# The last 128 tokens of a two-product kernel, computed and stored in three column parts

## The chip, the cores and the metric

The kernel runs on one core of a Trainium2 chip. A core has five engines that run side by side: TensorE (matrix products), VectorE, ScalarE, GpSimd and SyncE (called SP here, which does nothing in this kernel but issue transfers). They share a memory of 128 partitions (SBUF). TensorE writes its results to a second small memory, PSUM, from which VectorE or ScalarE copy them out. Transfers (DMAs) between SBUF and the chip's main memory are issued by an engine's queue and carried out by 16 DMA engines. The metric is the device time of one execution in microseconds (us). Five runs of the kernel before took 341.65 to 343.1 us, with a median of 342.26.

## The reference

The computation is an attention whose keys and values begin with a few extra "beacon" rows, followed by a two-layer network with a squared ReLU:

```
k_all = concatenate([beacon_k, k]); v_all = concatenate([beacon_v, v])
a     = softmax(scale * q @ k_all^T, causal over k)        # 8 batches, 8 heads, 576 rows, 64 wide
x     = (a @ v_all), heads side by side                    # 4608 tokens x 512
h     = x @ w_in                                           # first product, 512 -> 2048
g     = relu(h) ** 2
out   = g @ w_out                                          # second product, 2048 -> 512, float32
```

The output has 4608 rows (tokens) of 512 columns.

## The kernel before

The network's part goes through the 4608 tokens in nine chunks of 512 (`TCH`, `NCH`). The function `add_chunk(j)` describes the work of chunk `j` as a list of operations. In the first product (line 845) 16 groups of four matmuls each give 128 of the 2048 hidden columns for 512 tokens. ScalarE or VectorE apply the ReLU to each group (lines 861 and 863), and VectorE squares two of them at a time (line 870) into the tile `g`. The second product (line 880) takes four token tiles of 128 tokens. Each is the sum of 16 matmuls of 128x512 in one PSUM bank (`ps`), in four quarters (`qd`) of four matmuls. Each matmul has a weight load of its own, since the weights are the 128 tokens of `g`, and the 512 columns of `w_out` are what streams past them. The bank is then copied to the tile `osb` (the operation `ev`, which the function `copy_on` gives as line 316 on ScalarE or line 318 on VectorE), and a store (`st`) is issued from SP. In all chunks but the end of the last, two token tiles go out in one store of 512 KB (line 908). The last two token tiles of the last chunk have a store of 256 KB each (line 906).

The order of all the work is worked out when the kernel is built. The class `Order` plays through a small model of the engines: each operation has engines it may run on, a duration, a priority (lower goes first), the operations it needs (`deps`), those that must merely have been started (`behind`), and perhaps a PSUM bank to take and later give back. At each moment, a free engine takes the ready operation of the lowest priority. An operation counts as seen by those that need it a little after its end (`LAT`, 0.2 us for TensorE). The instructions are then written out in that order, and each engine runs its own in it. What waits on what on the chip is derived from which data each instruction reads and writes.

The operations that the change concerns are these: the quarters `s2.{j}.{ts}.{qd}` have the priority `base + 100 + 4 * ts + qd` and need the quarter before; the copy `ev{j}.{ts}` has the priority -15 and may run on ScalarE or, if that is busy, VectorE; the store `st{j}.{ts}` has the priority -20 and runs on SP. There are four PSUM banks in the pool `ps`, and the tile `osb` has two buffers of two token tiles each. SP's queue carries all stores and, earlier in the kernel, most loads. ScalarE's queue issues only two loads, at the very start (line 513). Line 1007 stands for what closes the kernel: SP waits for the transfers, and the engines meet.

Of the kernel before, what the change touches and what calls it, by code (L numbers as in the profile page):

```python
# [45 lines left out]
class Order:  # L46
# [16 lines left out]
    def add(self, *a, **kw):  # L63
        op = Op(*a, **kw)
        op.need = [d for d in op.need if d is not None]
        self.ops.append(op)
        return op
# [126 lines left out]
def kernel(  # L194
# [11 lines left out]
    nc = tc.nc  # L206
# [8 lines left out]
    TCH = 512  # L215
    NCH = n_tokens // TCH
    NMC = d_model // 128
    NFT = d_ff // 128
# [5 lines left out]
    def sb(name, shape, dt):  # L224
        return pool.tile(shape, dt, name=name)
# [5 lines left out]
    w_out_sb = sb("w_out", [128, NFT, d_model], BF16)  # L231
# [36 lines left out]
    g = [sb(f"g{i}", [128, NFT, TCH], BF16) for i in range(2)]  # L268
    osb = [sb(f"osb{i}", [128, 2, d_model], FP32) for i in range(2)]
# [3 lines left out]
    ps = [psum.tile([128, 512], FP32, name=f"ps{i}") for i in range(4)]  # L273
# [16 lines left out]
    add = order.add  # L290
# [23 lines left out]
    def copy_on(e, dst, src):  # L314
        if e == "ACT":
            nc.scalar.copy(dst, src)  # L316
        else:
            eng[e].tensor_copy(dst, src)  # L318
# [237 lines left out]
    for pr, segs in enumerate(STREAM):  # L556
        off, at = {}, 0
        for c, t0, t1 in segs:
# [3 lines left out]
            while t0 < t1:  # L562
                n, o = divmod(PW * pr + at, 512)
                w = min(t1 - t0, 512 - o)
                PIECES[n].append((pr, c, t0, t0 + w, o))
                t0, at = t0 + w, at + w
# [183 lines left out]
    s2_ops = {}  # L750
# [4 lines left out]
    def feeds_of(lo, hi):  # L755
        return [o for o, l, h in fed if l < hi and h > lo]
# [44 lines left out]
    w_ops = {}  # L801
# [9 lines left out]
    def add_weights_out():  # L811
        for i in range(4):
# [4 lines left out]
                    in_=moe_w_out.rearrange("(c p) f -> p c f", p=128)[:, i * n:(i + 1) * n, :])]  # L817
            w_ops["out", i] = add(f"wout{i}", "POOL", 1.3, emit, prio=-90 + i, behind=[v_loads[1][4]] if i == 0 else [w_ops["out", i - 1]], dma=2.6)

    def add_chunk(j):  # L820
        base = 1.0e5 + 1000.0 * j
        G = g[j % 2]
        sq = []
        t0, t1 = j * TCH, (j + 1) * TCH
        wrap = t1 // RING * RING
        if j == 0 and NSPLIT:
            parts = [(0, SPLIT[0].hi), (SPLIT[0].hi, t1)]
        else:
            parts = [(t0, t1)]
        for n, (lo_, hi_) in enumerate(parts):  # L830
            s1_ops[lo_, hi_] = []
        for f in range(NFT // 2):
            sqs = []
            for n, (lo_, hi_) in enumerate(parts):
                spans = [(lo_, wrap), (wrap, hi_)] if lo_ < wrap < hi_ else [(lo_, hi_)]
                N = hi_ - lo_
                relus = []
                for ft in (2 * f, 2 * f + 1):
                    box = {}

                    def emit_s1(e, ft=ft, spans=spans, box=box):
                        h = ps[box["s1"].held[2]]
                        for lo, hi in spans:
                            for mc in range(NMC):
                                nc.tensor.matmul(h[:, lo - spans[0][0]:hi - spans[0][0]],  # L845
                                                 w_in_sb[:, mc, ft * 128:(ft + 1) * 128],
                                                 xT[:, mc, lo % RING:lo % RING + hi - lo],
                                                 start=(mc == 0), stop=(mc == NMC - 1))

                    s1 = add(f"s1.{j}.{ft}.{n}", "PE", 0.865 * N / TCH, emit_s1, prio=base + ft + 0.5 * n,  # L850
                             deps=feeds_of(lo_, hi_) + [w_ops["in", f // 2]]
                             + [s2_ops[j - 2, u] for u in range(4) if j >= 2],
                             take=("ps", "mlp"), pe_time=0.865 * N / TCH)
                    box["s1"] = s1
                    s1_ops[lo_, hi_].append(s1)

                    def emit_relu(e, ft=ft, lo=lo_ - t0, hi=hi_ - t0, box=box):
                        h = ps[box["s1"].held[2]][:, 0:hi - lo]
                        dst = G[:, ft, lo:hi]
                        if e == "ACT":  # L860
                            nc.scalar.activation(dst, h, AF.Relu, bias=0.0, scale=1.0)  # L861
                        else:
                            nc.vector.tensor_scalar(out=dst, in0=h, scalar1=0.0, scalar2=None, op0=ALU.max)  # L863

                    relus.append(add(f"relu{j}.{ft}.{n}", ("ACT", "DVE"), {"ACT": 0.2 + N / 1200.0, "DVE": 0.13 + N / 960.0},
                                     emit_relu, prio=-20.0, deps=[s1], give=s1))

                def emit_sq(e, f=f, lo=lo_ - t0, hi=hi_ - t0):
                    d = G[:, 2 * f:2 * f + 2, lo:hi]
                    nc.vector.tensor_tensor(out=d, in0=d, in1=d, op=ALU.mult)  # L870

                sqs.append(add(f"sq{j}.{f}.{n}", "DVE", 0.1 + 0.6 * N / TCH, emit_sq, prio=-10.0, deps=relus))
            sq.append(sqs)
        for ts in range(TCH // 128):
            prev, first = None, {}
            for qd in range(4):
                def emit_s2(e, ts=ts, qd=qd, first=first):
                    o = ps[first["s2"].held[2]]
                    for fc in range(4 * qd, 4 * qd + 4):
                        nc.tensor.matmul(o, G[:, fc, ts * 128:(ts + 1) * 128],  # L880
                                         w_out_sb[:, fc, :], start=(fc == 0), stop=(fc == NFT - 1))

                prev = add(f"s2.{j}.{ts}.{qd}", "PE", 0.865, emit_s2, prio=base + 100 + 4 * ts + qd,
                           deps=sq[2 * qd] + sq[2 * qd + 1] + [w_ops["out", qd], prev],
                           take=None if qd else ("ps", "mlp"), pe_time=0.865)
                first.setdefault("s2", prev)
            s2_ops[j, ts] = prev
            u = 2 * j + ts // 2
            last = u == 2 * NCH - 1

            def emit_ev(e, ts=ts, first=first, u=u):
                copy_on(e, osb[u % 2][:, ts % 2, :], ps[first["s2"].held[2]])

            deps = [prev]
            if u >= 2:
                deps += st_ops[u - 2]
            evs = evs if ts % 2 else []
            evs.append(add(f"ev{j}.{ts}", ("ACT", "DVE"), {"ACT": 0.62, "DVE": 0.66}, emit_ev, prio=-15.0, deps=deps,
                           give=first["s2"]))
            st_ops.setdefault(u, [])  # L900
            if last or ts % 2:
                def emit_st(e, u=u, ts=ts, last=last):
                    d = osb[u % 2]
                    if last:
                        t0 = u * 256 + 128 * (ts % 2)
                        nc.sync.dma_start(out=out[t0:t0 + 128, :], in_=d[:, ts % 2, :])
                    else:
                        nc.sync.dma_start(out=out[u * 256:u * 256 + 256, :].rearrange("(t p) d -> p t d", p=128), in_=d)

                st_ops[u].append(add(f"st{j}.{ts}", "SP", 0.65, emit_st, prio=-20.0, deps=evs[-1:] if last else evs,  # L910
                                     dma=0.7 if last else 1.4))

    st_ops = {}
# [6 lines left out]
    for b in range(B):  # L920
# [8 lines left out]
        for n, (x, c) in enumerate(([] if b < NPE else nat) + [("v", c) for c in range(NT)]):  # L929
            behind, sync = [], []  # L930
            if x == "v" and b == 0:
                pass
            elif x == "v" and b == 1 and c == 0:
                behind = [strided[1, 0, HP - 1, "q"]]
            elif b == 2 and n == 0:
                sync = [w_ops["out", 3]]
            elif b >= NPE and x == "v" and c == 0:
                for y in "qk":
                    add_trans(b, y, lp - 5.0)
                behind = trans[b, "q"] + trans[b, "k"]  # L940
# [19 lines left out]
        if b >= 1:  # L960
            for j in late:
                add_chunk(j)
            late = []
# [48 lines left out]
```

## Time and profile before

| | us |
|---|---|
| median of 5 runs | 342.26 |
| the profiled execution | 342.79 |
| its span, first to last instruction | 340.7 |
| TensorE busy | 331.6 (97% of the span) |
| ScalarE busy | 190.4 |
| VectorE busy | 171.5 |
| GpSimd busy | 91.4 |
| last stretch of the second product (line 880) | 323.00 to 336.83 |
| last copy out of PSUM (line 316) | 336.91 to 337.49 |

The profile is of one execution, taken by the hardware's own profiler. The difference between the execution's own time and the span (2.1 us) lies outside the first and last instruction. TensorE's clock was granted in full. The page of the profile lists groups of instructions by source line and engine: the output tile, the input tiles, the shapes, how many there were, the time in which one of them ran, the mean length in ns of one, and the idle time ahead of them with what ended it. Other views give the instructions of a stretch in order of time, the chain of work that ended last, followed back from the last instruction, and the packets that the DMA engines moved, in 40 slices of a stretch, with each queue's number of packets. Queue q1 is SP's and q10 is ScalarE's. A matmul's length in these views runs from its start to the end of its last column; since matmuls are pipelined, the distance between two starts is shorter than that.

### The profile page before, as it was taken

What the parts mean: (1) busy time and instruction counts of PE and PEld (TensorE: products, weight loads), DVE (VectorE), ACT (ScalarE), POOL (GpSimd) and SP (SyncE); (2) the same over time, 40 slices, a digit from 0 to 9 for tenths busy, and PEclk for the clock granted to TensorE, in tenths of its full rate; (3) what the DMA queues carried; (4) which work ended last, traced back from release to release, by engine and by line L of the source; (5) the groups of instructions that cost most, each with busy time, mean ns of one, the idle gap of its engine ahead of it and who ended that gap; (6) DMA issues with size and microseconds to landing.
All of it is one profiled execution on the core that took longest, in us unless ns stands there. A gap on an engine that the chain in (4) does not pass through costs nothing.

```text
span 340.7 us, 7674 instructions
## 1 busy us (share of the span) xinstructions
PE 331.6 (97%) x3123; PEld 184.8 (54%) x3165; DVE 171.5 (50%) x388; ACT 190.4 (56%) x269; POOL 91.4 (27%) x145
## 2 busy tenths in 40 slices
PE   8999999999999999999999999989999999999995
PEld 7687765544554554555468854545554544444442
DVE  4886876237556972586347644664265403301300
ACT  3976865377548745675557544674367216515711
POOL 9874803316404504051424041313000000000000
PEclk9999999999999999999999999999999999999999
DMA  8999989999999998899989994998310131011002
GB/s 144 210 195 218 202 138 203 224 244 212 193 213 239 183 192 166 180 236 184 186 167 228 186 204 98 238 220 161 99 62 2 34 99 62 0 63 62 0 32 93
DMA packets 143665, 51.72 MB, mean 152 GB/s; under 512 B 130670, under 2 KB 138382, under 8 KB 143630
## 3 DMA queue, kind: packets, MB, share of 16 engines
q1 hardware_dynamic: 135231, 42.25, 62.7%
q0 software_dynamic: 7904, 8.69, 15.0%
q8 instruction: 25, 0.41, 0.5%
q10 hardware_dynamic: 495, 0.30, 0.3%
q14 instruction: 10, 0.08, 0.1%
HBM read 37.22 MB, written 9.44 MB: 137 GB/s over the span
## 4 chain that ended last, share of the span: by engine, by line
PE 82%; DMA 10%; POOL 4%; SPq 2%; issue 1%; ACT 0%; DVE 0%; POOLq 0%; ACTq 0%
PE ps L880 34%; PE ps L845 32%; PE ps L715 7%; PE strip L611 7%; DMA qk_area<-in_k_dram 3%; DMA stg<-in_k_dram 2%; DMA stg<-in_v_dram 2%; DMA kT<-qk_area 2%; SPq L765 2%; POOL qk_area L440 1%; DMA stg<-in_q_dram 1%; PE ps L475 1%; PE ps L782 1%; POOL stg L362 1%; POOL w_in L807 0%
## 5 line engine op out<-in xcount | busy, mean ns | idle before, releaser
L845 PE MATMUL ps<-xT,w_in 128*128 128x512 bf16 (+3 forms) x689 | 132.7, 340 | 0.9 <-issue 0.2
L880 PE MATMUL ps<-w_out,g 128*128 128x512 bf16 x549 | 130.5, 379 | 1.7 <-issue 0.5
L620 ACT ACTIVATE pt<-strip 128x1024 bf16<-128x1024 f32 (+3 forms) x107 | 101.9, 1000 | 43.0 <-PE strip L611 42.6
L845 PEld LDWEIGHTS <-w_in 128*128 128x128 bf16 x704 | 65.5, 98 | 52.0 <-issue 1.1
L861 ACT ACTIVATE g<-ps 128x512 bf16<-128x512 f32 (+2 forms) x120 | 67.5, 563 | 44.5 <-PE ps L845 43.7
L870 DVE TENSOR_TENSOR g<-g 128x1024 bf16<-128x1024 bf16 (+2 forms) x80 | 52.8, 665 | 68.5 <-ACT g L861 67.6
L880 PEld LDWEIGHTS <-g 128*128 128x128 bf16 x576 | 52.5, 98 | 57.4 <-issue 1.7
L318 POOL CAST qk_area<-stg 128x512 bf16<-128x512 f32 (+2 forms) x60 | 39.5, 667 | 66.8 <-DMA stg<-in_q_dram 34.4
L318 POOL CAST vb<-stg 128x512 bf16<-128x512 f32 (+1 forms) x40 | 25.7, 649 | 70.9 <-DMA stg<-in_v_dram 51.0
L316 ACT COPY osb<-ps 128x512 f32<-128x512 f32 x27 | 15.8, 586 | 51.1 <-PE ps L880 43.3
L715 PEld LDWEIGHTS <-pt 128*128 128x128 bf16 (+1 forms) x960 | 35.7, 98 | 11.0 <-issue 1.9
L715 PE MATMUL ps<-vb,pt 128*128 128x65 bf16 (+1 forms) x960 | 39.8, 194 | 0.1
L689 DVE TENSOR_TENSOR pt<-pt,tri 128x512 bf16<-128x512 bf16 x64 | 30.8, 490 | 10.7 <-ACT pt L620 9.6
L611 PE MATMUL strip<-qT,kT 64*128 64x208 bf16 (+15 forms) x596 | 34.2, 239 | 0.8 <-DMA kT<-qk_area 0.8
L734 DVE TENSOR_TENSOR xn<-ps,rcp 128x320 bf16<-128x320 f32 (+2 forms) x64 | 31.5, 492 | 2.3
L611 PEld LDWEIGHTS <-kT 64*128 64x128 bf16 x596 | 19.0, 94 | 22.1 <-issue 18.8
L732 DVE RECIPROCAL rcp<-ps 128x5 f32<-128x5 f32 (+2 forms) x64 | 12.2, 191 | 35.8 <-PE ps L715 35.6
L863 DVE TENSOR_SCALAR g<-ps 128x512 bf16<-128x512 f32 (+2 forms) x40 | 23.5, 602 | 9.8 <-PE ps L845 8.0
L318 DVE COPY osb<-ps 128x512 f32<-128x512 f32 x9 | 6.2, 691 | 17.9 <-PE ps L880 17.7
L286 PE MATMUL ps<-g 128*128 128x256 bf16 (+1 forms) x83 | 11.0, 285 | 1.1 <-DVE warm L293 1.1
L362 POOL DMA_DIRECT2D stg<-in_v_dram x10 | 8.6, 866 | 5.5 <-DMA w_in<-in_moe_w_in_dram 4.0
L693 DVE TENSOR_TENSOR pt<-pt,tri 80x160 bf16<-80x160 bf16 x32 | 9.8, 307 | 0.0
(38 smaller groups left out, 72.8 us busy)
## 6 DMA issues: line engine op xcount, KB each, us to landing
out_dram<-osb SPq DMA_DIRECT2D x17, 512.0 KB, 3.8
stg<-in_q_dram SPq DMA_DIRECT2D x24, 256.0 KB, 5.1
stg<-in_k_dram SPq DMA_DIRECT2D x18, 256.0 KB, 5.1
stg<-in_v_dram SPq DMA_DIRECT2D x18, 256.0 KB, 4.9
w_in<-in_moe_w_in_dram POOLq DMA_DIRECT2D x4, 512.0 KB, 7.8
w_out<-in_moe_w_out_dram POOLq DMA_DIRECT2D x4, 512.0 KB, 11.3
stg<-in_v_dram POOLq DMA_DIRECT2D x6, 256.0 KB, 7.9
stg<-in_k_dram SPq DMA_DIRECT2D x6, 224.0 KB, 4.6
```

Source lines behind the costliest of these rows:

```text
L316: nc.scalar.copy(dst, src)
L318: eng[e].tensor_copy(dst, src)
L611: nc.tensor.matmul(st[:, hj, at:at + t1 - t0], kT[b % 2][hp, pr, 128 * c:128 * c + 128], qT[b % 2][hp, pr, t0:t1], start=True, stop=True,)
L620: nc.scalar.activation(pt[:, :, at:at + width], strips[qk.slots[s]][:, :, 0:width], AF.Exp, bias=0.0, scale=scale)
L689: nc.vector.tensor_tensor(out=d, in0=d, in1=tri[:, m0:m0 + m, :][:, None].to_broadcast([128, 2, m, 128]), op=ALU.min)
L715: nc.tensor.matmul(a[:, at + (t - tl[0]) * (D + 1):at + (t - tl[0] + 1) * (D + 1)], P[0:rr, hj, o:o + 128], vb[b % 2][0:rr, c, 2 * pr + hj ...
L734: nc.vector.tensor_tensor(out=xn[b % 2].rearrange("p t (h d) -> p h t d", d=D)[:, h0:h0 + nh, tl[0]:tl[0] + nt], in0=a[:, :, :, 0:D], in1= ...
L845: nc.tensor.matmul(h[:, lo - spans[0][0]:hi - spans[0][0]], w_in_sb[:, mc, ft * 128:(ft + 1) * 128], xT[:, mc, lo % RING:lo % RING + hi - lo],
L861: nc.scalar.activation(dst, h, AF.Relu, bias=0.0, scale=1.0)
L863: nc.vector.tensor_scalar(out=dst, in0=h, scalar1=0.0, scalar2=None, op0=ALU.max)
L870: nc.vector.tensor_tensor(out=d, in0=d, in1=d, op=ALU.mult)
L880: nc.tensor.matmul(o, G[:, fc, ts * 128:(ts + 1) * 128], w_out_sb[:, fc, :], start=(fc == 0), stop=(fc == NFT - 1))
```

## The change

A new function, `add_last`, takes the place of the operations of the last token tile of the last chunk. The 512 output columns are computed in three parts of 256, 128 and 128 columns. Each part is a sum of 16 matmuls in a PSUM bank of its own, again in four quarters. The quarters follow one another by `behind` and not by `deps`, and a part's first quarter follows the last quarter of the part before. The first part is copied out by ScalarE, the second by VectorE, the third by ScalarE. Each has a store of its own, of 128 rows by its columns; the first two are issued from SP, the last from ScalarE's queue. The other three token tiles are as before.

```diff
+    def add_last(j, ts, base, sq):
+        u = 2 * NCH - 1
+        for n, (lo, hi) in enumerate(((0, 256), (256, 384), (384, 512))):
+            prev, box = None, {}
+            for qd in range(4):
+                def emit_s2(e, qd=qd, lo=lo, hi=hi, box=box):
+                    o = ps[box["s2"].held[2]][:, 0:hi - lo]
+                    for fc in range(4 * qd, 4 * qd + 4):
+                        nc.tensor.matmul(o, G_of(j)[:, fc, ts * 128:(ts + 1) * 128],
+                                         w_out_sb[:, fc, lo:hi], start=(fc == 0), stop=(fc == NFT - 1))
+
+                prev = add(f"s2.{j}.{ts}.{qd}.{n}", "PE", 0.865 * (hi - lo) / 512, emit_s2,
+                           prio=base + 100 + 4 * ts + n + 0.1 * qd,
+                           deps=sq[2 * qd] + sq[2 * qd + 1] + [w_ops["out", qd]], behind=[o for o in (prev or s2_ops.get((j, ts)),) if o],
+                           take=None if qd else ("ps", "mlp"), pe_time=0.865 * (hi - lo) / 512)
+                box.setdefault("s2", prev)
+            s2_ops[j, ts] = prev
+            e_ = ("ACT", "DVE", "ACT")[n]
+
+            def emit_ev(e, lo=lo, hi=hi, box=box):
+                copy_on(e, osb[u % 2][:, ts % 2, lo:hi], ps[box["s2"].held[2]][:, 0:hi - lo])
+
+            ev = add(f"ev{j}.{ts}.{n}", e_, 0.15 + (hi - lo) / 1100.0, emit_ev, prio=-15.0, deps=[prev] + st_ops[u - 2], give=box["s2"])
+
+            def emit_st(e, n=n, lo=lo, hi=hi):
+                t0 = u * 256 + 128 * (ts % 2)
+                (nc.sync, nc.sync, nc.scalar)[n].dma_start(out=out[t0:t0 + 128, lo:hi], in_=osb[u % 2][:, ts % 2, lo:hi])
+
+            st_ops[u].append(add(f"st{j}.{ts}.{n}", ("SP", "SP", "ACT")[n], 0.65, emit_st, prio=-20.0, deps=[ev], dma=0.2))
...
         for ts in range(TCH // 128):
+            if j == NCH - 1 and ts == TCH // 128 - 1:
+                add_last(j, ts, base, sq)
+                continue
             prev, first = None, {}
```

More of the change, by code (lines that the diff above doesn't have):

```diff
@@ L818, in add_weights_out, with G_of @@
             w_ops["out", i] = add(f"wout{i}", "POOL", 1.3, emit, prio=-90 + i, behind=[v_loads[1][4]] if i == 0 else [w_ops["out", i - 1]], dma=2.6)
+    def add_last(j, ts, base, sq):
[22 more added lines that the diff above has]
+            st_ops[u].append(add(f"st{j}.{ts}.{n}", ("SP", "SP", "ACT")[n], 0.65, emit_st, prio=-20.0, deps=[ev], dma=0.2))
+    def G_of(j):
+        return g[j % 2]
     def add_chunk(j):
```

## The prediction

> **What bounds the kernel now.** I read the page first: TensorE is busy 97% of the span at full clock in every slice, so before the last chunk only TensorE time counts. The change touches nothing there. It touches the last 128 tokens, so I went to the chain of waits from 318 us on (start, length, what):
>
> ```profile
> 318.09 4.91 PE ps L845 x22
> 323.00 5.83 PE ps L880 x27
> 328.83 0.05 issue
> 328.88 7.95 PE ps L880 x36
> 336.83 0.02 issue
> 336.85 0.02 ACTq L316
> 336.87 0.04 issue
> 336.91 0.58 ACT osb L316
> ```
>
> TensorE runs without a hole to 336.83; then one ScalarE copy of 128x512 ends at 337.49. The order of time of the same stretch (start, length, engine, line) shows the copies and the two stores on SP:
>
> ```profile
> 336.03 0.58 ACT L316 COPY osb<-ps 128x512 f32<-128x512 f32 x1 [5.45 <-PE ps L880]
> 336.64 1.22 SPq L906 DMA_DIRECT2D out_dram<-osb  x2
> 336.91 0.58 ACT L316 COPY osb<-ps 128x512 f32<-128x512 f32 x1 [0.29 <-PE ps L880]
> ```
>
> The second store issues at 337.52 (one issue lasts 0.35, from the line's own rows) and takes 2.04 us from issue to landing. The DMA view from 337.3 to 340 us shows what moves then: only these two stores, 256 data packets of 2 KB, the last at 339.2; landing is at 339.56 and the end at 340.73.
>
> ```profile
> DMA  0026999988997301789999899930000000000000
> q1 hardware_dynamic: 288, 0.52, 51.3%
> out_dram<-osb SPq DMA_DIRECT2D x1, 256.0 KB, 2.0
> ```
>
> So after TensorE's end (call it 0) come 0.08 to the copy, 0.58 copy, 0.03 to the issue, 2.04 to landing, 1.17 of closing waits: 3.90 us in all, and 336.83 + 3.90 = 340.73. This chain, and nothing else, is what the change can shorten.
>
> **The order of the work after the change.** The planner counts a matmul group as seen 0.2 us after its end for whoever depends on it, so it alternates quarters of two token tiles: tile 0 with 1, tile 2 with 3. The trace agrees: tiles 2 and 3 are copied out at 336.03 and 336.91, 0.88 apart, one quarter of four matmuls. After the change the same rule alternates tile 2's quarters with those of the 256-column part; then come the two 128-column parts, each whole. Counting back from the new TensorE end: last part -0.89 to 0; middle part to -0.89; the 256 part to -1.78; tile 2 to -2.21.
>
> **TensorE.** Removed: 16 matmuls of 512 columns at 216 ns (3.46 us). Added: 16 of 256 and 32 of 128, with 32 more weight loads. For 256 columns the first product with mixed 240 and 272 has a row, for 128 the 65-column matmuls and the transposes, each with a weight load of its own:
>
> ```profile
> 26.49 2.78 PE L845 MATMUL ps<-xT,w_in 128*128 128x240 bf16 x24
> 54.59 0.43 PE L782 MATMUL ps<-ident,xn 112*128 112x112 bf16 x5
> 24.37 0.90 PE L715 MATMUL ps<-vb,pt 128*128 128x65 bf16 x24
> ```
>
> A stretch is its starts plus the length of its last matmul (0.27, 0.22, 0.19 us). So (2.78-0.27)/23 = 109 ns at 256 columns, (0.43-0.22)/4 = 53 ns at about 128, and (0.90-0.19)/23 = 31 ns at 65: weight loads keep up at twice the pace that 128 columns need. I take 55.5 ns, the median between starts of equal 128x128 transposes in the trace. Then 16 x 109 + 32 x 55.5 = 3.52 us: **+0.06**. Here a rule speaks against the change: the Trainium skill, "TensorE: Matmul & The Clock Gate", section "Back-to-back issue gap", says that a stream of load and matmul pairs sustains only about 81 ns per matmul at 128 columns. By that rule the 32 take 2.59 instead of 1.78 us, an estimate of +0.87 instead of +0.06, and nearly the whole gain is gone. The same sentence has 131 ns for 512 columns where this trace has 216, and the 31 ns row cannot stand beside an 81 ns floor of load pairs, so the row decides; the rule's end stays in the range.
>
> **Evictions.** The last copy goes from 512 to 128 columns. Rows of ScalarE copies out of PSUM:
>
> ```profile
> L316 ACT COPY osb<-ps 128x512 f32<-128x512 f32 x27 | 15.8, 586 | 51.1 <-PE ps L880 43.3 <-remote 5.5 <-PE ps L715 1.4
> L316 ACT COPY xT<-ps 128x336 bf16<-128x336 bf16 x2 | 0.9, 442 | 0.3 <-PE ps L782 0.3
> L316 ACT COPY xT<-ps 128x240 bf16<-128x240 bf16 x1 | 0.4, 367 | 0.0
> ```
>
> The slope from 240 to 512 is 219/272 = 0.805 ns a column, so 128 columns cost 277 ns: **-0.31** (bounds: -0.22 if it costs as much as 240 columns, -0.37 if length were in proportion beyond that). The other two are off the path. Tile 2's copy fills ScalarE from -2.13 to -1.55, so the 256-column copy (0.38) waits behind it and ends at -1.15; ScalarE is idle long before 0. VectorE's 128-column copy of the middle part, 0.28 by its 393 ns (240) and 689 ns (512) rows from PSUM, ends at -0.53; VectorE has had nothing since 324.4. Were that cover gone, the cost would be ScalarE's lateness past 0, at most the 0.38.
>
> **Stores.** SP issues tile 2 (-1.51), the 256 part (-1.12) and the middle part (-0.50), 0.35 each, so SP is free at each. The first has its data done about -1.51 + 0.83 + 0.85 = +0.17 and the others about +0.45 and +0.75 (0.81 to 0.85 from issue to first packet is measured, then the packets). The last store is issued by ScalarE at 0.08 + 0.28 + 0.03 = +0.39 and its packets start near +1.2, on idle DMA engines.
>
> Its cost against the old last store: ScalarE's issue. Its two DMAs at the start of the kernel took 0.66 and 0.33 us to issue; SP's first took 0.46 and its late ones 0.35. I take the second: **-0.02**, with +0.31 as the bad end (a cold queue). The data: 128 rows of 512 B in place of 2 KB, 8 to each of 16 engines. The late stores' 2 KB packets average 86 ns in the trace, and the 240 packets of 512 B that ScalarE's queue loaded at the start average 27 ns. 8 x (86-27) = **-0.47**. Bounds: 0 if a store's packet costs the same whatever its size, -0.60 if nearly all of it goes. A second rule bears on it: "DMA: Bandwidth & Descriptors", section "Measured (HBM→SBUF, 128 partitions, SWDGE, issued from GpSimd)", gives 0.95 us of DMA time for 64 KB, more than the 0.83 that the whole 256 KB store takes here from first to last packet. By it this term would be an estimate of +0.1 rather than -0.47. It is for another queue and direction, so I keep the packet row. The remaining about 1.2 us of a store (issue to first packet, last packet to landing) I leave unchanged.
>
> **The close.** SP waits on the store semaphores in a fixed list. In the trace, five of those waits stand between 339.58 and 339.82, 0.06 apart, because the last store's semaphore is early in the list. Semaphores are handed round in turn, one per transfer, so with two more stores the last one stands two places further on: **-0.12** (0 if it doesn't).
>
> **The sum:** +0.06 - 0.31 - 0.02 - 0.47 - 0.12 = -0.86 us. Span 340.73 to 339.87. The profiled execution took 342.79, 2.06 around its span, which would become 341.93; it lies 0.53 over the median of the runs, 342.26, so on the median the forecast is 341.4.
>
> **Rivals.** (1) The gain is eaten. If TensorE runs at 81 ns, -0.86 + 0.81 = -0.05: 342.2. If instead the queue is cold (+0.33) and small packets are not cheaper (+0.47), -0.06: the same. For it: no row here has 128-column matmuls of this product, nor any store of 512 B rows. Against: the 31 ns and 27 ns rows.
>
> (2) Slower: the three column stores write interleaved pieces of the same 128 rows of the output, and if the ordering of transfers takes them as overlapping, each waits for the landing of the one before. Place: SP's and ScalarE's issue. The 256 part issues at -1.12 and lands 1.70 later at +0.58; the middle issues at +0.61 and lands at +2.18; the last issues at +2.21 and lands 1.55 later at +3.76, where the old store landed at +2.73. That is +1.03, with +0.06 and -0.12 about +1.0, and 0.1 for two more waits: 343.4. It decides once the last store issues later than about +1.25. Against it: the old second store issues at 337.52 while the first is still under way, so stores of separate rows aren't chained; for it: no two stores here share rows.
>
> (3) It doesn't do what it says: something else ends last. The middle part's store lands near +1.1, the last near +1.9; the middle one would have to be 0.8 late, which no row suggests. Then the gain would be under 0.3: 342.0. I count it with (1).
>
> **How the numbers follow.** A measurement of this kernel tells about 0.3% (1.03 us) from no change. The worked case has 0.70, from 340.8 to 341.9 with the bounds and the scatter of the runs (341.65 to 343.1). Its centre lies just inside 0.3%, so half of it, 0.35, counts as faster, and 0.35 as the same. Rival 1 with 3 has 0.15: 0.13 the same, 0.02 slower. Rival 2 has 0.15, slower. So 0.35, 0.48, 0.17. The range from 340.8 to 343.2 leaves out about one in ten at each end, the upper one most of rival 2.
>
> **What would show it.** Right: 128-column matmuls 55 ns apart, the last ScalarE copy near 0.28 us, three stores on SP and one on ScalarE's queue, its landing under 1.6 us after issue, and about 3.0 us from TensorE's end to the span's. Wrong: the last stretch of 32 matmuls over 2.3 us; an issue on ScalarE over 0.5; a wait of a store on another store's landing; packets of 512 B over 60 ns.

## The result and the profile after

| | before | after |
|---|---|---|
| median, us | 342.23 (39 runs) | 340.89 (20 runs) |
| ratio to before, 95% interval | | 0.9963 (0.9951 to 0.9974) |
| the profiled execution, us | 342.79 | 341.79 |
| its span, us | 340.7 | 340.1 |
| execution less span, all runs, us | 2.02 to 2.26 | 1.66 to 1.75 |

The changed kernel is faster by 0.37%, on 342.23 us that is 1.27 us (0.89 to 1.68). The last row matters: part of the gain lies outside the span. Its values for the kernel before come from the 103 runs of it beside the experiments, which list their spans (to 0.1 us).

The chain of waits of the changed kernel, its end (start, length, what; line 916 is the old line 880, line 828 the column parts, line 846 their stores, line 942 the old line 906):

```profile
330.94 0.44 PE ps L828 x4
331.38 0.86 PE ps L916 x4
332.25 0.44 PE ps L828 x4
332.68 0.86 PE ps L916 x4
333.55 0.44 PE ps L828 x4
333.98 0.86 PE ps L916 x4
334.85 2.24 PE ps L828 x36
337.08 0.02 issue
337.11 0.27 ACT osb L316
```

The quarters of tile 2 and of the 256-column part alternate as worked out. The last stretch is the fourth quarter of the 256 part and the 32 matmuls of 128 columns: (2.24 - 4 x 0.109)/32 = 56 ns each. TensorE again runs without a hole. Since the two profiled executions reach the last stage at different times (323.00 and 323.18 us for the second product), only stretches inside the stage are compared.

The same stretch in order of time:

```profile
334.93 0.86 ACT L316 COPY osb<-ps 128x512 f32<-128x512 f32 x2 [4.17 <-PE ps L916]
335.54 0.35 SPq L942 DMA_DIRECT2D out_dram<-osb  x1
335.98 0.94 SPq L846 DMA_DIRECT2D out_dram<-osb  x2
336.27 0.29 DVE L318 COPY osb<-ps 128x128 f32<-128x128 f32 x1 [11.73 <-PE ps L828]
337.11 0.27 ACT L316 COPY osb<-ps 128x128 f32<-128x128 f32 x1 [1.32 <-PE ps L828]
337.40 0.37 ACTq L846 DMA_DIRECT2D out_dram<-osb  x1
```

No store waits for another's landing: SP issues its three at 335.54, 335.98 and 336.58, before the first of them has landed (337.60). The last copy is 0.27 long, where it was 0.58, and the last store issues from ScalarE's queue 0.03 after it.

The packets from 337.3 to 340 us, in 40 slices (q10 is ScalarE's queue):

```profile
DMA  9989994000000027984000000000000000000000
q1 hardware_dynamic: 222, 0.13, 15.5%
q10 hardware_dynamic: 144, 0.07, 8.2%
out_dram<-osb ACTq DMA_DIRECT2D x1, 64.0 KB, 1.6
```

The last store moves on idle engines, with a gap of about 0.5 us ahead of it. Its 128 data packets of 512 B average 27 ns (86 ns for those of 2 KB before) and lie between 338.28 and 338.63; it lands at 339.03, 1.63 us after its issue began, and the span ends 1.04 later.

### The profile page after: what moved, and what is told of

It is laid out like the page before. It is cut to its first block, busy times and chain, and to the rows that moved or that the text cites. A ratio compares the mean times of both kernels' runs of the same rounds, so it can differ in the third digit from the quotient of the medians.

```text
span 340.1 us, 7745 instructions
## 1 busy us (share of the span) xinstructions
PE 332.2 (98%) x3155; PEld 187.0 (55%) x3197; DVE 172.5 (51%) x389; ACT 190.3 (56%) x270; POOL 93.5 (27%) x145
## 4 chain that ended last, share of the span: by engine, by line
PE 87%; DMA 6%; POOL 4%; issue 1%; DVE 1%; ACT 0%; POOLq 0%; DVEq 0%
PE ps L916 35%; PE ps L878 34%; PE ps L715 8%; PE strip L611 7%; DMA qk_area<-in_q_dram 4%; DMA stg<-in_v_dram 2%; POOL qk_area L440 2%; PE ps L828 1%; POOL stg L362 1%; PE ps L782 1%; DVE g L903 1%; POOL w_in L807 0%; PE ps L475 0%; POOL vb L318 0%; POOL tri L302 0%
## 5 line engine op out<-in xcount | busy, mean ns | idle before, releaser
L916 PE MATMUL ps<-w_out,g 128*128 128x512 bf16 x533 | 127.5, 379 | 1.7 <-issue 0.5
L916 PEld LDWEIGHTS <-g 128*128 128x128 bf16 x560 | 51.0, 98 | 54.8 <-issue 1.7
L318 POOL CAST qk_area<-stg 128x512 bf16<-128x512 f32 (+2 forms) x60 | 41.3, 691 | 65.4 <-DMA stg<-in_q_dram 35.4
L316 ACT COPY osb<-ps 128x512 f32<-128x512 f32 (+2 forms) x28 | 15.8, 567 | 50.8 <-PE ps L916 41.8
L689 DVE TENSOR_TENSOR pt<-pt,tri 128x512 bf16<-128x512 bf16 x64 | 31.6, 503 | 10.1 <-ACT pt L620 8.9
L318 DVE COPY osb<-ps 128x512 f32<-128x512 f32 (+1 forms) x10 | 6.5, 651 | 30.5 <-PE ps L916 13.5
```

The lines of the kernel that those rows point to most:

```text
L689: nc.vector.tensor_tensor(out=d, in0=d, in1=tri[:, m0:m0 + m, :][:, None].to_broadcast([128, 2, m, 128]), op=ALU.min)
L916: nc.tensor.matmul(o, G[:, fc, ts * 128:(ts + 1) * 128], w_out_sb[:, fc, :], start=(fc == 0), stop=(fc == NFT - 1))
```

## The experiments

**Does the last store's queue matter?** The changed kernel, with all three stores from SP:

```diff
-                (nc.sync, nc.sync, nc.scalar)[n].dma_start(
+                nc.sync.dma_start(
-            ... ("SP", "SP", "ACT")[n], 0.65, emit_st ...
+            ... "SP", 0.65, emit_st ...
```

> The changed kernel with the last store issued from SP instead of ScalarE's queue. Main theory (the gain is the short copy, the small packets and the semaphore's later place; the queue is worth nothing): SP has been free since 0.17 us before TensorE's end, so the stretch from TensorE's end to the span's end stays within 0.05 us of the changed kernel's 2.99, and the time stays about 1.2 us under the kernel before. Rival (the separate queue carries part of the gain, since three issues on SP get in each other's way): 0.2 to 0.4 us longer than the changed kernel.

From TensorE's end to the span's end 2.96 us, against 3.01 in the changed kernel; ratio to before 0.9960 (0.9939 to 0.9981), median 341.12. The order of time shows the three issues in a row and the same short copy:

```profile
335.53 1.75 SPq L846 DMA_DIRECT2D out_dram<-osb  x3
336.66 0.27 ACT L316 COPY osb<-ps 128x128 f32<-128x128 f32 x1 [1.32 <-PE ps L828]
```

The last issue takes 0.33 on SP and the landing 1.59, against 0.37 and 1.63 on ScalarE's queue. The queue brings nothing; it costs some 0.04 us in the trace, too little for the times to show.

**The queue alone**, in the kernel before:

```diff
-                        nc.sync.dma_start(out=out[t0:t0 + 128, :], in_=d[:, ts % 2, :])
+                        (nc.scalar if ts % 2 else nc.sync).dma_start(out=out[t0:t0 + 128, :], in_=d[:, ts % 2, :])
```

(with the same choice in the planner's engine.)

> The kernel before, with only its last store (256 KB, after the whole 512-column copy) moved to ScalarE's queue. Main theory: no gain; 3.90 us from TensorE's end to the span's end, within 0.06 (issue 0.37 against 0.35). Rival (the queue carries the gain): 3.6 or less. On what lies outside the span (2.06 us before, 1.72 after): if that follows the length of TensorE's program, it stays at 2.06 here; if it follows the last transfer's queue, it is 1.7.

3.95 from TensorE's end, landing 2.07 after issue, issue 0.38; ratio 1.0003 (0.9984 to 1.0021). Outside the span 2.03 to 2.23. So neither the gain inside the span nor the one outside it comes from the queue.

**Two parts instead of three:**

```diff
-        for n, (lo, hi) in enumerate(((0, 256), (256, 384), (384, 512))):
+        for n, (lo, hi) in enumerate(((0, 384), (384, 512))):
-            e_ = ("ACT", "DVE", "ACT")[n]
+            e_ = ("DVE", "ACT")[n]
```

(stores from SP and from ScalarE's queue.)

> The changed kernel with two parts, 384 and 128 columns, in place of 256, 128 and 128: the first copied by VectorE and stored from SP, the last as in the changed kernel. Main theory (only the last part's size counts): 0.02 to 0.04 us less on TensorE, the same copy and landing, one place earlier in the list of semaphores (+0.06): from TensorE's end 3.05, the whole within 0.1 us of the changed kernel inside the span. Rival (the staircase of two small parts matters, because the large first part's store is still moving when the last begins): landing of the last store 1.8 us or more after its issue instead of 1.63.

Ratio 0.9969 (0.9950 to 0.9988), median 341.18; its interval overlaps that of the changed kernel. The trace has 3.21 from TensorE's end, 0.16 more than expected. Its chain says where a third of it is:

```profile
336.24 0.02 issue
336.26 0.02 ACTq L316
336.27 0.04 issue
336.31 0.27 ACT osb L316
```

ScalarE again has a wait instruction of its own ahead of the copy (the ACTq line, as in the kernel before), which the changed kernel does not have: 0.06. Landing took 1.71, 0.08 more than in the changed kernel: the rival's direction, but short of its 1.8. The first part's packets ended at 337.59, after the last store's had begun at 337.50, so they did meet. With one store fewer, three waits follow that of the last store (two in the changed kernel), and the close takes 1.10, 0.06 more. TensorE's stretch is 0.04 shorter. In all, the staircase of small parts is worth 0.16 us in the trace, and a small last part alone keeps about four fifths of the gain inside the span.

**The size of the store alone**, in the kernel before:

```diff
-                        nc.sync.dma_start(out=out[t0:t0 + 128, :], in_=d[:, ts % 2, :])
+                        lo = 384 if ts % 2 else 0
+                        nc.sync.dma_start(out=out[t0:t0 + 128, lo:], in_=d[:, ts % 2, lo:])
```

> The kernel before with the last store cut to columns 384 to 511 (the other 384 columns of the last 128 tokens are left unstored); matmuls, copy and queue are unchanged. Main theory (2 KB packets cost 86 ns, 512 B ones about 27 to 35): landing 1.6 us after issue instead of 2.04, and 3.45 from TensorE's end to the span's end instead of 3.90. Rival (64 KB takes as long as 256 KB[...]): 2.0 and 3.9.

Landing 1.65 us after issue, 3.53 from TensorE's end; ratio 0.9987 (0.9971 to 1.0002). The packets of the last store, from 337.2 to 338 us in 40 slices of 0.02:

```profile
DMA  0001237899998957642000000000000000000000
q1 hardware_dynamic: 145, 0.07, 28.2%
```

They are done in about 0.35 us. 28.2% of 16 engines' 0.8 us over 145 packets is 25 ns each, and 27 for the 128 data packets alone (the other 17 hold 4 bytes). The rival, that 64 KB takes as long as 256 KB, is out: the store's part of the gain is 0.39 in this run, with queue, copy and TensorE unchanged.

**What saves 0.35 us outside the span?** Three kernels had shown it so far: all runs of the changed kernel (1.66 to 1.75), of the one with SP's stores (1.68 to 1.78) and of the one with two parts (1.66 to 1.76) are under 1.8, all runs of the others are over 2.0. The first guess was TensorE's program, which has 64 instructions more. The padding splits filler matmuls at the start, where TensorE is idle:

```diff
-        nc.tensor.matmul(ps[bank][:, 0:cols], g[1][:, 0, 0:128], g[1][:, 0, 0:cols], start=True, stop=True)
+        k = 2 if len(split) < 32 else 1
+        split.append(bank)
+        for at in range(0, cols, cols // k):
+            nc.tensor.matmul(ps[bank][:, at:at + cols // k], g[1][:, 0, 0:128], g[1][:, 0, at:at + cols // k], start=True, stop=True)
```

> The kernel before with the first 32 of its filler matmuls at the start (TensorE's idle time there) each split into two of half the width: 64 more TensorE instructions, as many as the change adds, nothing else on any engine. Theory (the 0.35 us that the changed kernel saves outside the span comes from the length of TensorE's program, which moves where its closing code lies): outside the span 1.7 us as in the changed kernel, inside it 340 to 341 with 3.91 from TensorE's end; the time 0.2 to 0.5 us under the kernel before. Rival (it comes from VectorE's or ScalarE's few new instructions or from the last transfer): still about 2.06, and no change in time.

> As the run with 64, with 64 fillers split: 128 more TensorE instructions than before. If what counts is the place within a block of 128 instructions[...], this is where the kernel before is: 2.06 outside the span. If the block is 256 long or the effect is of length alone: 1.7.

> As the run with 64, with 42 fillers split into four and two into two: 256 more TensorE instructions than before. A block of 128 or of 256 gives 2.06 outside the span; an effect of length alone gives 1.7.

> The changed kernel with the first 32 fillers split in two: 64 more TensorE instructions than the change has, 128 more than before. If a block of 128 counts: outside the span 2.06 again, 3.0 from TensorE's end to the span's end as in the changed kernel, and so only 0.84 us under the kernel before, 341.4. If not: 1.7 and 341.0.

| kernel | TensorE instructions more than before | execution less span, all runs | from TensorE's end | ratio to before |
|---|---|---|---|---|
| before, +64 | 64 | 2.02 to 2.14 | 3.91 | 1.0018 (0.9999 to 1.0038) |
| before, +128 | 128 | 2.01 to 2.13 | 3.93 | 1.0019 (0.9999 to 1.0040) |
| before, +256 | 256 | 2.04 to 2.20 | 3.92 | 0.9991 (0.9973 to 1.0010) |
| changed, +64 | 128 | 1.66 to 1.76 | 3.02 | 0.9976 (0.9961 to 0.9992) |

The guess fell: the length of TensorE's program does nothing to it. (The changed kernel with padding was 0.82 us under the kernel before, where 1.2 had been expected if the guess fell; its interval, 0.27 to 1.33, holds both.) It had to be something else that the column parts bring, and all kernels that saved it had a VectorE copy near the end. Three more runs separate VectorE's late work from its longer program.

```diff
# the kernel before, last copy on VectorE
-            evs.append(add(f"ev{j}.{ts}", ("ACT", "DVE"), ...
+            evs.append(add(f"ev{j}.{ts}", "DVE" if last and ts % 2 else ("ACT", "DVE"), ...
# the kernel before, one VectorE instruction more at the start
     nc.vector.memset(warm, 0.0)
+    nc.vector.memset(warm, 0.0)
# the changed kernel, middle part's copy on ScalarE
-            e_ = ("ACT", "DVE", "ACT")[n]
+            e_ = "ACT"
```

> The kernel before with one change: the very last copy out of PSUM (512 columns) is made by VectorE instead of ScalarE. All that saved 0.35 us outside the span so far have a VectorE copy in the last microsecond of TensorE's work, and all that didn't have none. Theory (VectorE, idle since 324.4 us, is what the close waits for when it has long slept): outside the span 1.7 us; inside it the copy is 0.69 instead of 0.585, so 4.0 from TensorE's end; in sum about 0.25 us under the kernel before. Rival A (the length of VectorE's program, one instruction longer): 1.7 as well. Rival B (the number of transfers or ScalarE's extra instructions): 2.06.

> The kernel before with one VectorE instruction more at its very start (a second clearing of a 128x8 tile) and VectorE as idle at the end as before. Theory (late work): 2.06 outside the span, time as before. Rival A (length of VectorE's program): 1.7 and 0.35 us less.

> The changed kernel with the middle part's copy on ScalarE instead of VectorE, which then does nothing after 324.4 us, as before the change. ScalarE is free from 1.1 us before TensorE's end, and the copy of 128 columns is done 0.5 before it, so the last copy is not delayed: 3.0 from TensorE's end. Theory (and rival A): 2.06 outside the span, 0.84 instead of 1.2 under the kernel before, 341.4. Rival B: 1.7 and 341.0.

| kernel | VectorE instructions more than before | VectorE's last work | execution less span, all runs | from TensorE's end | ratio to before |
|---|---|---|---|---|---|
| before, last copy on VectorE | 1, with two waits | last us | 1.66 to 1.82 | 3.96 | 1.0003 (0.9985 to 1.0020) |
| before, +1 on VectorE | 1 | as before | 1.67 to 1.79 | 3.92 | 0.9997 (0.9981 to 1.0012) |
| changed, middle on ScalarE | 0 | as before | 2.06 to 2.12 | 3.01 | 0.9968 (0.9954 to 0.9982) |

The second row decides against late work: VectorE sleeps there as it does in the kernel before, and one clearing of 0.07 us at its start is enough. The order of time shows it as one of two on the tile `warm`, where the kernel before has one:

```profile
1.02 0.07 DVE L293 MEMSET warm<- 128x8 f32 x1
1.16 0.07 DVE L294 MEMSET warm<- 128x8 f32 x1
```

The third row is the counterpart: the changed kernel without a VectorE copy of its own keeps its 3.01 inside the span and loses the 0.35 outside. So the number of VectorE's instructions decides which of the two values comes. The ratios of the first two rows do not show the 0.35, which is 0.1% and less than their intervals; it is shown by the execution's time less its span, where no run of the one kind reaches the other.

The last run asks whether it is a place in a short block:

```diff
         order.run()
+        for _ in range(16):
+            nc.vector.memset(warm, 0.0)
```

> The kernel before with 16 clearings of a 128x8 tile at the end of VectorE's program, where VectorE has nothing to do for 16 us: 16 instructions more and no time inside the span (3.9 from TensorE's end). One more instruction gave 1.7 us outside the span, and so did the three more of the column parts. If what counts is the place of VectorE's end within a block of 16 instructions or a divisor of it: 2.06 to 2.1. If a longer block or the length itself counts: 1.7.

1.67 to 1.84 outside the span, 3.93 from TensorE's end, ratio 0.9984 (0.9961 to 1.0008). The added instructions do lie where VectorE has nothing else to do:

```profile
322.70 0.69 DVE L870 TENSOR_TENSOR g<-g 128x1024 bf16<-128x1024 bf16 x1 [1.04 <-ACT g L861]
323.34 2.07 DVE L983 MEMSET warm<- 128x8 f32 x16
```

A block of 16 or a divisor of 16 is out; a longer block and a simple threshold are both left.

The traces hold one more thing that moves with VectorE's program: the last packet of the kind "instruction" on queue q14. These are the packets after the span's end, before (340.7 to 343 us) and changed (340.1 to 343), in 40 slices:

```profile
DMA  0000000000000000000000000000040000000000
q14 instruction: 1, 0.01, 1.1%
DMA  0000000000002000000000000000000000000000
q14 instruction: 1, 0.01, 0.7%
```

It starts 1.61 to 1.67 us after the span's end in all seven kernels with as many VectorE instructions as before, TensorE's padding or not. It starts at 1.35 with one more, at 0.62 to 0.91 with three more, and with 16 more at 322.56, 17.2 us before the end and just before the added clearings run. So it seems to belong to a fixed place of VectorE's instructions, which they reach during the close in most of these kernels, and ahead of it with 16 more. That it causes the 0.35 is not shown: in the kernel before it starts at 1.67, later than the work of the close that is late there (1.14, in the last section). Why the close depends on the length stays open.

No version beat the changed kernel by more than the runs can tell.

## Why the prediction was right, and what it missed

The order of the work, the place of the gain and its mechanism were as forecast, and the median 340.89 lies in the range of 340.8 to 343.2, near its lower end. But the worked case was a gain of 0.86 us, just within 0.3%, with more chance on no change (0.48) than on a gain past 0.3% (0.35), and the measured gain is 1.27. Its excess comes from a term that was put at nothing. The range holds the median by only 0.09 us, and that is in part luck, since its width was meant for other causes. Term by term, from the two traces:

| term | forecast | measured |
|---|---|---|
| TensorE, second product of the last chunk | +0.06 | +0.08 (13.98 to 14.06, first start to last end) |
| from TensorE's end to the last copy | 0 | -0.05 |
| last copy | -0.31 | -0.32 (0.585 to 0.265) |
| last store, issue to landing | -0.49 | -0.41 (2.04 to 1.63) |
| closing waits inside the span | -0.12 | -0.13 (1.17 to 1.04) |
| around the span | 0 | about -0.37 (medians 2.08 to 1.71) |
| sum | -0.86 | -1.20 |

**TensorE.** The row of 65-column matmuls decided rightly: the 32 matmuls came at 56 ns, against the 81 ns of the Trainium skill ("TensorE: Matmul & The Clock Gate", section "Back-to-back issue gap"). By that rule the stretch of 36 would have been, as an estimate, 3.03 us long instead of 2.24.

**The copy and the handover.** 265 ns against the 277 from the slope (the outer bound for this term, from a length in proportion to the columns below 240, comes to -0.39 and not -0.37). The 0.05 ahead of it was not foreseen: the kernel before has a separate wait instruction on ScalarE (the ACTq line of its chain), the changed one doesn't. Why it has none was not looked into.

**The store.** The packets cost 27 ns, as taken from the loads at the start, and 8 x (86 - 27) is the forecast 0.47. From issue to landing the gain was 0.41, 0.06 less than that; 0.02 of this is the issue on ScalarE's queue, which took 0.37 where SP's took 0.35 and 0.33 was forecast. The landing, 1.63 after the issue, so just missed the "under 1.6 us" named as a sign of being right; the other signs came. The other end, the 0.95 us for 64 KB by another queue and direction (the Trainium skill, "DMA: Bandwidth & Descriptors", section "Measured (HBM→SBUF, 128 partitions, SWDGE, issued from GpSimd)"), does not hold for this store: its data took 0.35. The queue itself, forecast at -0.02, costs 0.04.

**The close.** The last store's semaphore (the counter that tells of its landing) did move two places on. SP's waits from its landing on, before and after (line 1043 is the old line 1007):

```profile
L1007 SPq EVENT_SEMAPHORE  x5: 28/28/28, 339.6 to 339.8; - x5
L1043 SPq EVENT_SEMAPHORE  x3: 28/28/28, 339.1 to 339.2; - x3
```

After its own wait come two others, where four came before. With two parts it was three, and the close took 1.10, between the 1.17 before and the 1.04 here.

**The step that failed** is the one ahead of the forecast, "2.06 around its span, which would become 341.93": the sum carried the time around the span over unchanged. It fell by about 0.37, a side effect of a longer VectorE program (the middle part's copy and its waits) and not of any of the change's aims. With it, -1.20 agrees with the measured gain of 1.27 (0.89 to 1.68); without it, the 0.83 of the other terms lies just outside that interval.

**The rivals.** TensorE at the slower pace did not happen, nor dear packets or a cold queue, nor a chain of stores: at 337.40, when the last was issued, three were under way on the same rows. Something else ending last was not seen either: the middle part's store landed 0.85 us before the last one.

## What to carry to other kernels

What follows the last matmul is a chain of copy, issue, data and landing, and only what scales with the last piece can be cut: here a quarter of the columns took 0.32 off the copy and 0.4 off the store for 0.08 on TensorE, and the queue it went out from was worth nothing. Price small pieces by rows of the same trace with the same packet size and with a weight load for each matmul; such rows existed here, far from the stage in question. Where a few tenths of a us are at stake, compare the execution's time less its span as well: it can move with the length of an engine's program, and a stage's own reading will not show it.

## What the runs showed of the hardware that was not expected

The time outside the span is 2.01 to 2.26 us in every run of the kernels whose VectorE program is as long as before, and 1.66 to 1.84 in every run of those with 1, 3 or 16 VectorE instructions more (by the trace's count, waits included), whether VectorE works late or sleeps for 16 us before the end. 64, 128 and 256 instructions more on TensorE leave it as it is. After the kernel's last instruction the traces show the semaphores from 7 to 255 updated one after another, which looks like their clearing. Semaphores 207 to 255 have their turn at 0.65 us after the span's end in both kernels. The others start at 1.14 in the kernel before and at 0.77 in the changed one, and this shift of 0.37 is as large as the difference outside the span.
